# mLSTM attention feeding an FFN on one core: selection a slot earlier, exponents queued behind squares and x copies, state product and splits queued behind y

## The chip, the cores and the metric

The kernel runs on one core of a Trainium2 chip. The metric is device time of one execution in microseconds (us). The engines are named as in the profile: PE (TensorE, matmuls), PEld (its weight loads), DVE (VectorE), ACT (ScalarE), POOL (GpSimd) and SP (SyncE, whose queue issues the DMAs). A line such as L80 in a row of the profile is the line of a helper that issues the instruction, so the tiles' names tell the rows apart.

## The reference

Two steps follow each other. The first is a recurrent attention (mLSTM) over 4 batches, 8 heads, 768 positions and a head size of 40. For each position it does

```python
m_new = max(f + m, i)
C = exp(f + m - m_new) * C + exp(i - m_new) * outer(v, k)
n = exp(f + m - m_new) * n + exp(i - m_new) * k
y = sigmoid(o) * (C @ q) / max(abs(n . q), 1)
```

The second takes y, laid out as x with 3072 tokens of 320 columns, through `h = x @ w_in` (320 x 2048), a gate `g` that is h where h >= 1, 0 where h <= -1 and (h + 1)^2 / 4 between, and `g @ w_out` (2048 x 320).

## The kernel before

**Attention.** The positions are cut into 6 chunks of 128. A block n is one batch of one chunk, n = 4 * chunk + batch, so there are 24 blocks. Within a chunk the recurrence becomes matmuls: a decay matrix per head, made from sums of gates, is multiplied with the scores k.q, and the product with v; what came before the chunk enters through the state C. The work of a block is written as generators, which the program advances by a slot each:

- `prep(n)` (line 475): `select` sets the upper triangle of the block's tile Abc (128 x 8 heads x 128) to -30000 with an affine_select on POOL. `decay(n, hh)` (line 492) then takes the exponents of four heads, hh = 0 and 1, on ACT, eight instructions of 128x128 in all. `scale1` makes v1 on POOL, and the next block's v is loaded.
- `score(n)`: eight matmuls into two tiles psa, each multiplied into Abc by DVE; v2 on POOL.
- `main(n)` (line 569): PE multiplies the state with qn, DVE makes hv from it, then PE multiplies Abc with v1. For n >= 8, but not for the last batch of a chunk, both are first split into three bf16 parts by `parts3` (line 149): DVE writes what is left of v1 (v3) and of Abc (m3) after the first part, POOL what is left after the second, and PE does 96 small matmuls. DVE adds up into hv. Here `load_A(n + 3)` issues the load of a later block's Abc from a_d; the tiles Abc have three buffers. In the next slot DVE does z (two steps), its reciprocal, sz and y, and `carry_on` (line 544) makes the next state: PE multiplies v2 and k into psa, DVE masks the product into a tile C, POOL decays the old C, DVE adds the two. In a last slot PE transposes y, ACT casts it to xh, and DVE writes the rest to xl and to rows of xh.

**FFN.** The x of four blocks, one chunk, is X[j] with 512 tokens. An iteration x = 16 * j + fc takes one group of 128 of the 2048 columns. `mm1` does eight matmuls into psh (two buffers); ACT takes a Relu and a square into r; DVE makes r the gate, which frees psh. `parts` casts r to gh on ACT and writes the rest to gl on DVE. Two iterations later `mm2` does up to twelve matmuls from gh and gl into the four tiles pso. The iteration x = 16 * j can't begin before the last block of chunk j has been cast to xh; so x = 32 and x = 48 wait for the blocks 11 and 15. Its outputs are copied out by ACT and DVE.

**What sets the order.** The program calls the slots of the attention between the FFN's iterations: `plan` (line 643) puts prep, score and main of a block at slots that a list OFFS gives, 4 (LEAD) slots ahead of the score for prep and 3 (MLAG) behind it for main. A chunk's sigmoid of the output gate is called at its first main. Within this a scheduler sets each engine's queue. `behind(...)` (line 416) adds edges to it: an instruction issued under `behind("r", "act")` stands on its engine behind the last instruction that was marked so. The marks that exist before are ("r", "act"), the last square on ACT; ("r", "dve"), the last gate on DVE; ("x", "act"), the last cast to xh; ("x", "dve"), the last rest; and ("v", "pool"). An edge bears only on the order in a queue; each engine runs its own queue in order. The pool of tiles psa has two buffers, that of Abc three.

Of the kernel before, what the change touches and what calls it, by code (L numbers as in the profile page):

```python
# [13 lines left out]
ALU = mybir.AluOpType  # L14
# [3 lines left out]
B, H, S, D = 4, 8, 768, 40  # L18
D1 = D + 1
# [23 lines left out]
LEAD = 4  # L43
MLAG = 3
NA = 3
ST = 0


# [48 lines left out]
def mlstm_ffn_kernel(ctx, tc, qk, qn, vk, og, fi0, fi, w_in, w_out, cst, out):  # L97
    nc = Core(tc)
# [24 lines left out]
    bmask = cs_t.rearrange("p (g x) -> p g x", g=3)  # L123
# [25 lines left out]
    def parts3(x, name, eng):  # L149


        halves = lambda w: w.bitcast(BF16).rearrange("p h (t w) -> p h t w", w=2)
        hi = halves(x)[:, :, :, 1]
        rest = late.tile(list(x.shape), F32, name=name, bufs=1)
        eng[0].tensor_tensor(out=rest, in0=x, in1=hi, op=ALU.subtract)
        mid, lo = halves(rest)[:, :, :, 1], halves(rest)[:, :, :, 0]
        eng[1].tensor_tensor(out=lo, in0=rest, in1=mid, op=ALU.subtract)
        return hi, mid, lo
# [231 lines left out]
    mark = {}  # L390
# [25 lines left out]
    def behind(*names, only=True):  # L416
        es = ExitStack()
        for k in names:
            if only and k in mark:
                es.enter_context(tc.issue_after(mark[k].ins))  # L420
        return es
# [53 lines left out]
    def prep(n):  # L475

        c, b = divmod(n, B)
        t = T[n]
        select(n)
        for hh in range(2):  # L480
            decay(n, hh)
            yield
        scale1(n)
        load_v(n + 1)
        yield

    def select(n):
        A = T[n]["A"]
        nc.gpsimd.affine_select(out=A, in_=A, pattern=[[0, H], [1, L]], compare_op=ALU.is_ge,
                                fill=-30000.0, base=0, channel_multiplier=-1)  # L490

    def decay(n, hh):

        c, b = divmod(n, B)
        A = T[n]["A"]
        for h in range(4 * hh, 4 * hh + 4):
            bias = nA[:, c, b * H + h:b * H + h + 1]
            src = T[n]["Ap"][hh][:, (h - 4 * hh) * L:][:, :L] if c == 0 else A[:, h, :]
            nc.scalar.activation(A[:, h, :], src, AF.Exp, bias=bias)
# [44 lines left out]
    def carry_on(n, t):  # L544

        c, b = divmod(n, B)
        kp = psum_a()
        for gi, h0 in enumerate(GROUPS):
            nc.tensor.matmul(kp[0:120, gi * 3 * D1:(gi + 1) * 3 * D1], t["kn"][:, h0 * D:(h0 + 3) * D],
                             t["v2"][:, h0:h0 + 3, :], start=True, stop=True)  # L550
        Cn = st.tile([120, 3, 3 * D1], F32, name="C", bufs=5)
        nc.vector.tensor_tensor(out=Cn, in0=kp[0:120, :9 * D1].rearrange("p (g x) -> p g x", g=3),
                                in1=bmask, op=ALU.mult)
        if c > 0:
            C = state[b]
            nc.gpsimd.tensor_tensor(out=C, in0=C, in1=dec[:, :, b, c:c + 1].broadcast_to([120, 3, 3 * D1]),
                                    op=ALU.mult)
            nc.vector.tensor_tensor(out=Cn, in0=Cn, in1=C, op=ALU.add)
        state[b] = Cn
# [9 lines left out]
    def main(n):  # L569

        c, b = divmod(n, B)
        t = T.pop(n) if n >= B else T[n]
        g = gates_of(n)
        sg = sig[c][:, b, :]
        M = t["A"]
        if c > 0:
# [6 lines left out]
            hv = wk.tile([P, H, D1], F32, name="hv", bufs=2)  # L583
# [4 lines left out]
        if n < SPLIT_FROM or b == B - 1:  # L588
            for h in range(H):
                nc.tensor.matmul(up[:, h * D1:(h + 1) * D1], M[:, h, :], t["v1"][:, h, :], start=True, stop=True)  # L590
        else:
            prod = [(i, k) for i in range(3) for k in range(3 - i)]
            v = parts3(t["v1"], "v3", (nc.vector, nc.gpsimd))
            for h in range(H):
                if h % 8 == 0:
                    m = parts3(M[:, h:h + 8, :], "m3", (nc.vector, nc.gpsimd))
                for i, k in prod:
                    nc.tensor.matmul(up[:, h * D1:(h + 1) * D1], m[i][:, h % 8, :], v[k][:, h, :],
                                     start=((i, k) == (0, 0)), stop=((i, k) == (2, 0)))
# [3 lines left out]
        else:  # L603
            hv = uv
# [8 lines left out]
        sz = wk.tile([P, H, D], F32, name="sz", bufs=1)  # L613
        nc.vector.tensor_tensor(out=sz, in0=sg.rearrange("p (h d) -> p h d", d=D),
                                                     in1=z.unsqueeze(2).broadcast_to([P, H, D]), op=ALU.mult)
        y = wk.tile([P, DM], F32, name="y", bufs=2)
        nc.vector.tensor_tensor(out=y.rearrange("p (h d) -> p h d", d=D), in0=hv[:, :, 0:D], in1=sz, op=ALU.mult)
        if 0 < c < NC - 1:
            carry_on(n, t)
        yield  # L620
# [8 lines left out]
        j, r = divmod(n, NTC)  # L629
        if r == 0:  # L630
# [8 lines left out]
                                op=ALU.subtract)  # L639
# [4 lines left out]
    for n in range(NS):  # L644
        j, r = divmod(n, NTC)
        s0 = FRONT + OFFS[n - B] if j else 0
        if j:
            todo = ("prep", s0 - (LEAD if j > 1 else LEAD - 1), 3), ("score", s0, 2), ("main", s0 + MLAG, 3)
        else:
            todo = ("first", FRONT + ST + n, 2),  # L650
        for kind, i0, k in todo:
            for i in range(k):
                plan.setdefault(i0 + i, []).append((n, kind))
# [241 lines left out]
```

## Time and profile before

| | |
|---|---|
| time, median of three runs (lowest to highest) | 540.07 us (538.07 to 540.72) |
| the profiled execution's own time | 538.07 us |
| its span, from the first to the last instruction | 536.3 us |
| granted PE clock, mean | 0.958 of full speed |
| PE waits for psh, from DVE r | 12.2 us in 4 waits, longest 6.8 |
| PE waits for psa, from DVE y | 4.5 us in 2 waits, longest 2.3 |
| PE waits for psa, from DVE xh | 2.4 us in 2 waits, longest 1.9 |
| PE waits for psh, from ACT xh | 1.9 us in 2 waits, longest 0.9 |
| PE's share of the chain that ended last | 75% |

The rows that the prediction quotes are of three kinds. A row of a timeline reads: start in us, length in us, engine, line, operation, tile written <- tiles read, shapes, count, and in brackets the idle time of the engine just before it with what ended it. Instructions of one kind that follow each other share a row. A row of the table by stretches reads: the stretch, its length, the busy time (and number of instructions) of PE, PEld, DVE, ACT and POOL in it, then the granted clock of PE, the busy share of the DMA engines and GB/s. The page's first line gives busy time, its share of the span, and the number of instructions of each engine.

### The profile page before, as it was taken

Reading aid. Unit: us, or ns where it says so; the run is one execution under the profiler, and the core shown is the slowest. Engines: PE = TensorE matmul, PEld = TensorE weight load, DVE = VectorE, ACT = ScalarE, POOL = GpSimd, SP = SyncE. Lnnn points to the kernel's source line nnn. Section 1 sums busy time; section 2 is a strip of 40 time slices with the busy share of each in tenths; the row PEclk is TensorE's granted clock in tenths of the full one; section 3 lists DMA queues with packets and bytes.
Section 4 is the critical chain, followed back from the end, with each engine's and each line's share of the span. In section 5 each row is a group of like instructions: output and inputs, shape, how many; then the busy total and the mean of one; then the engine's idle time right before and its main releaser. Section 6 shows DMA issues by size and latency. Waiting matters only on the chain.

```text
span 536.3 us, 8899 instructions
## 1 busy us (share of the span) xinstructions
PE 501.1 (93%) x3396; PEld 427.1 (80%) x3399; DVE 359.7 (67%) x669; ACT 291.5 (54%) x576; POOL 138.8 (26%) x140
## 2 busy tenths in 40 slices
PE   8957999798997999969999979999999999999996
PEld 5735777676786889958888967988988889989986
DVE  5799997678675687748567558885566755544342
ACT  6544964555267464546636527663668444446553
POOL 3147423233352132223131232431231310000000
PEclk9987999899797999988999988999999999999999
DMA  8859454442441123233221233322243000010001
GB/s 245 264 188 303 129 172 146 149 153 91 142 134 19 41 63 103 79 88 93 51 87 56 80 113 120 74 90 77 68 149 135 19 1 2 0 38 13 1 1 50
DMA packets 29647, 51.30 MB, mean 96 GB/s; under 512 B 10124, under 2 KB 20004, under 8 KB 29604
## 3 DMA queue, kind: packets, MB, share of 16 engines
q1 hardware_dynamic: 29604, 50.72, 30.5%
q8 instruction: 27, 0.44, 0.4%
q14 instruction: 16, 0.13, 0.1%
HBM read 46.67 MB, written 4.04 MB: 95 GB/s over the span
## 4 chain that ended last, share of the span: by engine, by line
PE 75%; DVE 7%; ACT 7%; issue 3%; POOL 3%; DMA 3%; SPq 0%; ACTq 0%; POOLq 0%; DVEq 0%
PE psh L80 31%; PE pso L80 27%; PE psa L80 13%; ACT Abc L80 3%; POOL Abc L80 2%; PE psa L83 2%; DMA Abc<-a_d 2%; ACT r L80 1%; PE pso L83 1%; POOL v L80 1%; DVE r L80 1%; PE psh L83 1%; DVE win L80 1%; DVE ow L80 1%; DMA wraw<-in_w_out 1%
## 5 line engine op out<-in xcount | busy, mean ns | idle before, releaser
L80 ACT ACTIVATE r<-psh,half 128x512 f32<-128x512 f32 x96 | 65.2, 684 | 103.2 <-PE psh L80 102.9
L80 PE MATMUL psh<-xh,wh 128*128 128x512 f32 x288 | 107.4, 429 | 14.8 <-DVE r L80 12.2
L80 DVE SCALAR_TENSOR_TENSOR r<-psh,r 128x512 f32<-128x512 f32 x96 | 65.7, 686 | 80.6 <-ACT r L80 80.0
L80 PE MATMUL psh<-xh,wl 128*128 128x512 f32 x288 | 103.6, 414 | 0.0
L80 PE MATMUL pso<-ow,gh 128*128 128x320 f32 x320 | 99.4, 313 | 0.0
L80 PE MATMUL pso<-oh,gh 128*128 128x320 f32 x320 | 99.3, 313 | 0.0
L80 PE MATMUL pso<-oh,gl 128*128 128x320 f32 x320 | 93.3, 313 | 0.0
L80 DVE TENSOR_TENSOR gl<-r,gh 128x512 fp32r<-128x512 f32 x80 | 60.5, 758 | 32.4 <-ACT gh L80 31.9
L80 ACT CAST gh<-r 128x512 fp32r<-128x512 f32 x80 | 49.5, 618 | 48.9 <-DVE r L80 48.5
L80 PEld LDWEIGHTS psh<-xh,wh 128*128 128x128 f32 x288 | 53.1, 199 | 24.9 <-DVE r L80 13.9
L80 ACT ACTIVATE Abc<-Abc,nA 128x128 f32<-128x128 f32 x160 | 49.3, 390 | 37.3 <-POOL Abc L80 37.3
L80 PEld LDWEIGHTS psh<-xh,wl 128*128 128x128 f32 x288 | 56.7, 199 | 14.0 <-DVE m L83 0.4
L80 PEld LDWEIGHTS pso<-ow,gh 128*128 128x128 f32 x320 | 60.7, 190 | 3.4
L80 PEld LDWEIGHTS pso<-oh,gh 128*128 128x128 f32 x320 | 60.7, 190 | 3.3
L80 PE MATMUL psh<-xl,wh 128*128 128x512 f32 x192 | 62.7, 410 | 0.0
L80 ACT ACTIVATE r<-r 128x512 f32<-128x512 f32 x96 | 60.2, 631 | 2.4
L80 PEld LDWEIGHTS pso<-oh,gl 128*128 128x128 f32 x320 | 58.2, 188 | 0.8
L80 POOL TENSOR_TENSOR v<-vk,G 128x328 f32<-128x328 f32 x36 | 29.7, 829 | 67.2 <-issue 43.7
L80 PEld LDWEIGHTS psh<-xl,wh 128*128 128x128 f32 x192 | 37.6, 197 | 8.5
L80 POOL TENSOR_TENSOR C<-C,dec 120x369 f32<-120x369 f32 x16 | 13.7, 856 | 111.0 <-PE psa L80 111.0
L80 PE MATMUL pso<-ow,r 128*128 128x320 f32 x128 | 39.3, 452 | 0.0
L80 DVE TENSOR_TENSOR Abc<-psa,Abc 128x512 f32<-128x512 f32 x40 | 25.9, 680 | 17.8 <-PE psa L80 17.8
(187 smaller groups left out, 728.2 us busy)
## 6 DMA issues: line engine op xcount, KB each, us to landing
Abc<-a_d SPq DMA_DIRECT2D x20, 512.0 KB
raw<-in_qk SPq DMA_DIRECT2D x48, 160.0 KB
vk<-in_vk SPq DMA_DIRECT2D x20, 324.0 KB
wraw<-in_w_in SPq DMA_DIRECT2D x8, 768.0 KB
wraw<-in_w_out SPq DMA_DIRECT2D x8, 640.0 KB
sig<-in_og SPq DMA_DIRECT2D x6, 640.0 KB
out<-r SPq DMA_DIRECT2D x24, 160.0 KB
qn<-in_qn SPq DMA_DIRECT2D x20, 180.0 KB
```

The source lines that it names most:

```text
L80: r = getattr(self.engine, name)(*args, **kwargs)
L83: r = getattr(self.engine, name)(*args, **kwargs)
```

## The change

Blocks 4 to 7 (JOINED) keep their selection and exponents in one slot. For all other blocks `prep` starts a slot earlier and does only the selection in its first slot, so that the exponents keep their slots. The exponents are issued behind the last square and the last cast to xh on ACT. The masked state product and the splits v3 and m3 are issued behind the last y on DVE.

```diff
--- before.py
+++ after.py
@@ -43,6 +43,8 @@
 LEAD = 4
 MLAG = 3
 NA = 3
+
+JOINED = (4, 5, 6, 7)
 ST = 0
 
 
@@ -477,8 +479,11 @@
         c, b = divmod(n, B)
         t = T[n]
         select(n)
+        if n not in JOINED:
+            yield
         for hh in range(2):
-            decay(n, hh)
+            with behind(("r", "act"), ("x", "act")):
+                decay(n, hh)
             yield
         scale1(n)
         load_v(n + 1)
@@ -549,8 +554,9 @@
             nc.tensor.matmul(kp[0:120, gi * 3 * D1:(gi + 1) * 3 * D1], t["kn"][:, h0 * D:(h0 + 3) * D],
                              t["v2"][:, h0:h0 + 3, :], start=True, stop=True)
         Cn = st.tile([120, 3, 3 * D1], F32, name="C", bufs=5)
-        nc.vector.tensor_tensor(out=Cn, in0=kp[0:120, :9 * D1].rearrange("p (g x) -> p g x", g=3),
-                                in1=bmask, op=ALU.mult)
+        with behind("y"):
+            nc.vector.tensor_tensor(out=Cn, in0=kp[0:120, :9 * D1].rearrange("p (g x) -> p g x", g=3),
+                                    in1=bmask, op=ALU.mult)
         if c > 0:
             C = state[b]
             nc.gpsimd.tensor_tensor(out=C, in0=C, in1=dec[:, :, b, c:c + 1].broadcast_to([120, 3, 3 * D1]),
@@ -590,10 +596,12 @@
                 nc.tensor.matmul(up[:, h * D1:(h + 1) * D1], M[:, h, :], t["v1"][:, h, :], start=True, stop=True)
         else:
             prod = [(i, k) for i in range(3) for k in range(3 - i)]
-            v = parts3(t["v1"], "v3", (nc.vector, nc.gpsimd))
+            with behind("y"):
+                v = parts3(t["v1"], "v3", (nc.vector, nc.gpsimd))
             for h in range(H):
                 if h % 8 == 0:
-                    m = parts3(M[:, h:h + 8, :], "m3", (nc.vector, nc.gpsimd))
+                    with behind("y"):
+                        m = parts3(M[:, h:h + 8, :], "m3", (nc.vector, nc.gpsimd))
                 for i, k in prod:
                     nc.tensor.matmul(up[:, h * D1:(h + 1) * D1], m[i][:, h % 8, :], v[k][:, h, :],
                                      start=((i, k) == (0, 0)), stop=((i, k) == (2, 0)))
@@ -614,7 +622,7 @@
         nc.vector.tensor_tensor(out=sz, in0=sg.rearrange("p (h d) -> p h d", d=D),
                                                      in1=z.unsqueeze(2).broadcast_to([P, H, D]), op=ALU.mult)
         y = wk.tile([P, DM], F32, name="y", bufs=2)
-        nc.vector.tensor_tensor(out=y.rearrange("p (h d) -> p h d", d=D), in0=hv[:, :, 0:D], in1=sz, op=ALU.mult)
+        mark["y"] = nc.vector.tensor_tensor(out=y.rearrange("p (h d) -> p h d", d=D), in0=hv[:, :, 0:D], in1=sz, op=ALU.mult)
         if 0 < c < NC - 1:
             carry_on(n, t)
         yield
@@ -645,7 +653,8 @@
         j, r = divmod(n, NTC)
         s0 = FRONT + OFFS[n - B] if j else 0
         if j:
-            todo = ("prep", s0 - (LEAD if j > 1 else LEAD - 1), 3), ("score", s0, 2), ("main", s0 + MLAG, 3)
+            lead = (LEAD if j > 1 else LEAD - 1) + (n not in JOINED)
+            todo = ("prep", s0 - lead, 3 + (n not in JOINED)), ("score", s0, 2), ("main", s0 + MLAG, 3)
         else:
             todo = ("first", FRONT + ST + n, 2),
         for kind, i0, k in todo:
```

What this does to the queues is shown at three places. In the rows a number behind a name tells the tiles of one name apart; the numbers of later tiles differ by up to three between the two kernels.

The first is ACT around x = 32, before. Abc_2130 is block 14, xh_1615 the x of chunk 2 (its fourth cast is block 11's), r_2365 belongs to x = 32, sig_2132 is chunk 3's output gate, and x8 counts instructions of one kind in a row:

```order
L80 ACTIVATE ex_2162<-ah_2160 32x128
L80 ACTIVATE Abc_2130<-Abc_2130,nA_122 128x128 x8
L80 CAST xh_1615<-psa_2231 128x3x128
L80 ACTIVATE r_2365<-psh_2356,half_118 128x512
L80 ACTIVATE r_2403<-psh_2394,half_118 128x512
L80 COPY r_2498<-pso_1379 128x320
L80 ACTIVATE r_2365<-r_2365 128x512
L80 ACTIVATE r_2403<-r_2403 128x512
L80 ACT_TABLE_LOAD
L80 ACTIVATE sig_2132<-sig_2132 128x1280
L80 CAST gh_2375<-r_2365 128x512
```

and after:

```order
L82 CAST xh_1615<-psa_2231 128x3x128
L82 ACTIVATE Abc_1989<-Abc_1989,nA_122 128x128 x8
L82 ACTIVATE r_2365<-psh_2356,half_118 128x512
L82 ACTIVATE r_2406<-psh_2397,half_118 128x512
L82 COPY r_2498<-pso_1379 128x320
L82 ACTIVATE r_2365<-r_2365 128x512
L82 ACTIVATE r_2406<-r_2406 128x512
L82 ACT_TABLE_LOAD
L82 ACTIVATE sig_2132<-sig_2132 128x1280
L82 ACT_TABLE_LOAD
L82 ACTIVATE Abc_2130<-Abc_2130,nA_122 128x128 x4
L82 CAST gh_2378<-r_2365 128x512
```

The cast of block 11's x no longer stands behind eight exponents. Abc_1989 (block 13) now stands behind it, and half of block 14's exponents behind the sigmoid, with a table load between, ahead of the cast gh_2378.

The second is DVE ahead of x = 32, before. C_2190 is the state after block 11, v3 belongs to block 12, and hv, z, sz and y to block 11:

```order
L80 SCALAR_TENSOR_TENSOR ah_2160<-rst_128,fi_t_2157 32x128
L80 TENSOR_TENSOR gl_2334<-r_2321,gh_2332 128x512
L80 TENSOR_TENSOR hv_2118<-psa_2120,hv_2118 128x328
L80 TENSOR_TENSOR C_2190<-psa_2186,cs_99 120x369
L80 TENSOR_TENSOR v3_2414<-v1_2194 128x328
L80 SCALAR_TENSOR_TENSOR z_2178<-hv_2118,G_121 128x8
L80 TENSOR_TENSOR C_2190<-C_2190,C_1297 120x369
L80 TENSOR_TENSOR z_2178<-z_2178,hv_2118 128x8
L80 RECIPROCAL z_2178<-z_2178 128x8
L80 TENSOR_TENSOR sz_2182<-sig_1241,z_2178 128x320
L80 TENSOR_TENSOR y_2184<-hv_2118,sz_2182 128x320
L80 TENSOR_TENSOR xl_1616<-psa_2231,xh_1615 128x2x128
```

and after:

```order
L82 TENSOR_TENSOR hv_2118<-psa_2120,hv_2118 128x328
L82 SCALAR_TENSOR_TENSOR ah_2160<-rst_128,fi_t_2157 32x128
L82 TENSOR_TENSOR gl_2334<-r_2321,gh_2332 128x512
L82 SCALAR_TENSOR_TENSOR z_2178<-hv_2118,G_121 128x8
L82 TENSOR_TENSOR z_2178<-z_2178,hv_2118 128x8
L82 RECIPROCAL z_2178<-z_2178 128x8
L82 TENSOR_TENSOR sz_2182<-sig_1241,z_2178 128x320
L82 TENSOR_TENSOR y_2184<-hv_2118,sz_2182 128x320
L82 TENSOR_TENSOR C_2190<-psa_2186,cs_99 120x369
L82 TENSOR_TENSOR v3_2417<-v1_2194 128x328
L82 TENSOR_TENSOR C_2190<-C_2190,C_1297 120x369
L82 TENSOR_TENSOR xl_1616<-psa_2231,xh_1615 128x2x128
```

hv moves ahead of a scan (ah) and of gl_2334; the mask of C, v3 and the addition of C move from ahead of z, sz and y to behind y.

The third is ACT at the start of attention chunk 2, before. sig_1241 is its output gate, Abc_1239 block 10, Abc_1494 block 11, and gh_1407 the first cast behind the sigmoid:

```order
L80 ACT_TABLE_LOAD
L80 ACTIVATE sig_1241<-sig_1241 128x1280
L80 CAST oh_133<-ow_611 128x640
L80 CAST gh_1407<-r_1397 128x512
L80 COPY r_1521<-pso_533 128x320
L80 CAST gh_1504<-r_1428 128x512
L80 ACTIVATE ex_1269<-ah_1267 32x128
L80 ACT_TABLE_LOAD
L80 ACTIVATE Abc_1494<-Abc_1494,nA_122 128x128 x3
L80 ACTIVATE r_1539<-psh_1530,half_118 128x512
L80 ACTIVATE Abc_1494<-Abc_1494,nA_122 128x128 x5
L80 ACTIVATE r_1539<-r_1539 128x512
```

and after:

```order
L82 ACTIVATE sig_1241<-sig_1241 128x1280
L82 ACT_TABLE_LOAD
L82 ACTIVATE Abc_1239<-Abc_1239,nA_122 128x128 x4
L82 CAST oh_133<-ow_611 128x640
L82 CAST gh_1410<-r_1397 128x512
L82 COPY r_1521<-pso_533 128x320
L82 CAST gh_1504<-r_1431 128x512
L82 ACTIVATE ex_1269<-ah_1267 32x128
L82 ACTIVATE r_1539<-psh_1530,half_118 128x512
L82 ACTIVATE r_1604<-psh_1595,half_118 128x512
L82 ACTIVATE r_1539<-r_1539 128x512
L82 ACTIVATE Abc_1239<-Abc_1239,nA_122 128x128 x4
```

A table load and four exponents of block 10 stand directly behind the sigmoid, ahead of the casts of oh and of gh. The exponents of block 11 are gone from between this chunk's Relu and square of r_1539, and the other four of block 10 stand in their place, behind that square.

Elsewhere: the eight exponents of block 9 move from ahead of a Relu (r_1363) to behind two later casts of xh. At the start of chunk 4 four exponents stand ahead of the second square and four behind sigmoid and table load; at that of chunk 5 eight. At the start of x = 48 the same holds for C, v3 and y of block 15 as for block 11. On DVE at the start of chunk 2, y, v3, m3 and C stand ahead of the gate of r_1539, where C and y stood behind it. On POOL the selection passes the low part of v3. On SP some loads swap places.

## The prediction, made before the run

> **What bounds the kernel now.** The page's busy times come first. They name the bound:
>
> ```profile
> PE 501.1 (93%) x3396; PEld 427.1 (80%) x3399; DVE 359.7 (67%) x669; ACT 291.5 (54%) x576; POOL 138.8 (26%) x140
> ```
>
> Of a span of 536.3 us TensorE is busy for 501.1, so it stands idle for 35.2, and no change of order can give more than this and whatever busy time runs at a low clock. The second view is the table by stretches, which shows the granted clock (the last figure but two) beside PE's busy time:
>
> ```profile
> 133.20:140.00 6.80, 6.80 (x23) 5.37 (x23) 5.96 (x12) 0.08 (x1) 3.62 (x4) 0.50 0.46 149
> 164.00:170.80 6.80, 5.99 (x18) 5.19 (x19) 5.96 (x13) 4.44 (x9) 0.20 (x1) 0.50 0.04 8
> 228.80:232.20 3.40, 1.33 (x7) 0.96 (x8) 1.36 (x3) 2.81 (x9) 0.11 (x1) 1.00 0.50 137
> 232.20:235.60 3.40, 3.40 (x10) 2.63 (x9) 0.30 (x2) 0.00 (x0) 0.00 (x0) 0.50 0.15 56
> 239.10:242.50 3.40, 2.22 (x15) 1.61 (x14) 3.40 (x4) 3.37 (x6) 3.16 (x2) 1.00 0.72 227
> 242.50:245.90 3.40, 3.40 (x10) 2.57 (x9) 2.61 (x8) 2.40 (x5) 1.05 (x2) 0.50 0.16 52
> 317.60:321.00 3.40, 3.30 (x8) 2.62 (x9) 0.72 (x2) 0.05 (x1) 0.00 (x0) 0.50 0.33 123
> 327.80:331.20 3.40, 3.40 (x18) 2.92 (x16) 3.36 (x9) 3.37 (x6) 0.15 (x1) 0.50 0.28 88
> 340.00:410.00 70.00, 70.00 (x553) 62.10 (x552) 47.76 (x89) 41.45 (x84) 18.90 (x20) 1.00 0.29 96
> ```
>
> From 340 to 410 us PE is busy all the time at clock 1.00, so nothing can be won there. Before that there are stretches of 3.4 us, or two of them, at clock 0.50. Those whose forerunner is shown follow a stretch in which PE stood idle for over a microsecond: 2.07 of 3.40 us before 232.20, 1.18 before 242.50. A stretch at half clock does half its work, so it costs 1.7 us, and a double one 3.4. An idle gap is thus paid twice where it is long enough.
>
> A page of the Trainium skill, "TensorE: Matmul & The Clock Gate", section "HAM oscillation — how this bites in real kernels", gives the rule that PE should have no idle gaps over about 3.4 us. By it most of these stretches would have no cause; the trace does not agree, since 1.18 us of idle time in a stretch of 3.4 was followed by the half clock, and I go by the trace.
>
> The third view is PE's timeline around two starts of a chunk of tokens, x = 32 and x = 48, where new x must be ready before the FFN can go on:
>
> ```profile
> 227.44 0.31 PE L80 MATMUL pso<-oh,gl 128*128 128x320 f32 x1
> 229.92 0.52 PE L80 MATMUL psa<-ident,y 128*128 128x128 f32 x3 [2.17 <-DVE y L80]
> 231.80 0.88 PE L80 MATMUL psh<-xh,wh 128*128 128x512 f32 x2 [0.94 <-ACT xh L80]
> 315.83 0.52 PE L80 MATMUL psa<-ident,y 128*128 128x128 f32 x3 [2.31 <-DVE y L80]
> 317.70 1.22 PE L80 MATMUL psh<-xh,wh 128*128 128x512 f32 x2 [0.94 <-ACT xh L80]
> ```
>
> At both PE waits twice: for y (2.17 and 2.31 us), then for the cast of x to xh (0.94 each). Between the waits lie only the transposes and two score matmuls.
>
> **The change, part by part.** No instruction's kind or size changes, and the ACT_TABLE_LOADs of the order stay 12. All that moves is queue order.
>
> *y ahead of the state product and the splits, at x = 32.* DVE's and ACT's rows there:
>
> ```profile
> 223.66 0.41 DVE L80 TENSOR_TENSOR_SCAN ah<-rst,fi_t 32x128 f32<-32x128 f32 x1
> 224.12 1.03 DVE L80 TENSOR_TENSOR gl<-r,gh 128x512 fp32r<-128x512 f32 x1
> 225.08 0.48 DVE L80 TENSOR_TENSOR hv<-psa,hv 128x328 f32<-128x328 f32 x1
> 225.49 0.53 DVE L80 TENSOR_TENSOR C<-psa,cs 120x369 f32<-120x369 f32 x1
> 225.93 0.48 DVE L80 TENSOR_TENSOR v<-v 128x328 f32<-128x328 f32 x1
> 226.42 0.53 DVE L80 TENSOR_TENSOR C<-C 120x369 f32<-120x369 f32 x1
> 229.28 0.49 DVE L80 TENSOR_TENSOR y<-hv,sz 128x320 f32<-128x320 f32 x1
> 228.94 2.45 ACT L80 ACTIVATE Abc<-Abc,nA 128x128 f32<-128x128 f32 x8 [4.52 <-POOL Abc L80]
> 231.29 0.45 ACT L80 CAST xh<-psa 128x384 fp32r<-128x384 f32 x1
> ```
>
> Neighbours overlap by some 0.08 (v3 starts 0.44 after C, which is 0.53 long), so C mult, v3 and C add take 0.53 + 0.48 + 0.53 less 0.24: 1.30. The changed order also puts hv ahead of the scan and of gl, 223.66 to 225.08: 1.42. Together y ends 2.72 earlier, at 229.77 − 2.7 = 227.1. PE is done with its own work at 227.75, so the wait of 2.17 goes. Then comes the cast. Before, it starts as the eight exponents release ACT (228.94 + 2.45 = 231.39), although the transposes were over at 230.44. In the changed order these exponents (block 14) stand a chunk start later, and the ones that stand here (block 13) come behind the cast. So the cast follows the transposes at once and lies beside the two score matmuls. Transposes and score matmuls took PE from 229.92 to 231.80 − 0.94 = 230.86, that is 0.94; 227.75 + 0.94 is 228.7 for the first psh, against 231.80: −3.1. The idle time left in that stretch is under 0.3, below the 1.18 that was followed by half clock, so the stretch at 232.20 should run at full clock: −1.7. What is late next is the C product, behind y: it starts at about 227.1 in place of 225.49 and holds a psa buffer 1.6 longer; the score matmuls want that buffer at 228.2, when it is free by half a microsecond, so I count nothing; if that cover is gone it costs at most those 1.6.
>
> *The same at x = 48.* 317.70 becomes 314.55 by the same steps (2.31 + 0.94, less 0.1 of remaining wait): −3.15, and the stretch at 317.60: −1.7.
>
> *Block 9's exponents.* At 129 us they hold ACT before Relu and the xh cast:
>
> ```profile
> 126.52 2.44 ACT L80 ACTIVATE Abc<-Abc,nA 128x128 f32<-128x128 f32 x8 [1.53 <-POOL Abc L80]
> 130.72 0.47 ACT L80 CAST xh<-psa 128x384 fp32r<-128x384 f32 x1
> 129.15 0.49 PE L80 MATMUL psa<-ident,y 128*128 128x128 f32 x3
> 132.20 2.02 PE L80 MATMUL psa<-v,Abc 128*128 128x41 f32 x13 [1.93 <-DVE xh L80]
> ```
>
> Afterwards they stand behind this xh cast and the next. The Relu, square and cast between them then move up by up to 2.44, but the xh cast can't start before the transposes end at 129.64, so it gains 130.72 − 129.67 = 1.05 of the 1.93. An idle rest of 0.88 is less than the 1.18 seen, yet the half clock of 133.20 to 140.00 is open, so its 3.4 goes into the range and not into the sum: −1.05.
>
> *Exponents behind squares, at the three starts of attention chunks 2, 3 and 4.* Here the new order speaks against the change. ACT at the start of chunk 2, and what PE takes from it:
>
> ```profile
> 152.15 1.28 ACT L80 ACT_TABLE_LOAD   x1
> 153.44 1.28 ACT L80 ACTIVATE sig<-sig 128x1280 f32<-128x1280 f32 x1
> 155.24 0.62 ACT L80 CAST gh<-r 128x512 fp32r<-128x512 f32 x1
> 157.19 0.31 PE L80 MATMUL pso<-oh,gh 128*128 128x320 f32 x1
> 164.81 1.22 PE L80 MATMUL psh<-xh,wh 128*128 128x512 f32 x2 [3.30 <-DVE r L80]
> ```
>
> Behind the sigmoid now stand a table load and four exponents, ahead of the cast of gh. A load is 1.28 by its row, four exponents half of 2.44 to 2.45, so 1.25: gh is ready 2.5 later, at 158.4, where PE wants it at 157.2. A new wait of 1.2 is born. But the eight exponents of block 11 no longer stand ahead of the square of the next r. A copy, a gh, an ex, two Relus and the square follow at some 0.5 each (gh is 0.62 long), so ACT has that square by about 161.4. DVE, whose last gl waits for the second gh, reaches y at about 161.0 and has y, v3, m3 and C ahead of r: by the rows above 0.49, 0.48 and 0.53, and some 1.4 for m3, which has three times v3's columns; 161.0 + 2.8 + 0.6 for r is 164.4 where PE could go on at 164.81. The two waits together are 0.4 shorter: −0.4 net, and between −3.3, if DVE's order is kinder, and +1.2, if only the new wait is left over. The half clock from 164.00 stays.
>
> The Trainium skill's page "ScalarE: Activation LUTs", section "What ACT_TABLE_LOAD costs", puts a switch at about 2.66 us, 1.28 for the load and 1.38 for draining. By it three loads moved ahead of casts would cost up to 4.1 us more, and the sum below would be some 4 us smaller. The trace does not show that drain: sig starts 1.29 after the load, and I keep 1.28.
>
> The starts of chunks 3 and 4 look alike, with the casts and the matmuls that wait for them here:
>
> ```profile
> 243.31 0.60 ACT L80 CAST gh<-r 128x512 fp32r<-128x512 f32 x1
> 246.56 0.31 PE L80 MATMUL pso<-oh,gh 128*128 128x320 f32 x1
> 326.91 0.72 PE L80 MATMUL psh<-xh,wh 128*128 128x512 f32 x2 [1.26 <-DVE r L80]
> 329.14 0.60 ACT L80 CAST gh<-r 128x512 fp32r<-128x512 f32 x1
> 331.17 0.41 PE L80 MATMUL pso<-oh,gh 128*128 128x320 f32 x1
> ```
>
> Chunk 3: 243.91 + 2.5 is 246.4, at PE's 246.56. The first matmul is met, the next casts are as late and not all are: between 0 and 2.5, I take 1.0. Chunk 4: four more exponents stand ahead of the second square and the sigmoid, so gh ends at 329.74 + 3.8 = 333.5, where PE wants it at 331.17 and, with 0.7 of a longer wait at 326.91 behind m3, at 331.9. The two make 2.3; a score or state product in PE's queue fills some, so I take 1.9, between 0.7 and 2.5. The half clocks at 242.50 and 327.80 stay. At chunk 5 and at the FFN's later starts the same casts stand behind the same load and up to eight exponents (1.28 + 2.45 = 3.7), but they lie past 340 us, where PE never waits by the row above: between 0 and 3.7, I take 0, nearest to that row.
>
> *Selection a slot earlier.* It starts when its load has landed, not when it is issued:
>
> ```profile
> 151.64 0.33 SPq L80 DMA_DIRECT2D Abc<-a_d  x1
> 155.73 4.72 POOL L80 TENSOR_SCALAR_AFFINE_SELECT Abc<-Abc 128x1024 f32<-128x1024 f32 x1 [3.17 <-DMA Abc<-a_d]
> ```
>
> By itself it is worth nothing; in POOL's order it only passes the low part of v3. That part then ends later by a select, up to 4.7 us; the split products that read it stand later in PE's queue: nothing, at most the 1.0 that I already count at chunk 3.
>
> *Before 125 us* exponents move behind squares and Relus in the same way as for block 9, some with gain and some with loss: I count nothing, ±1.05 by block 9's term.
>
> **Sum.** −3.1 − 1.7 − 3.15 − 1.7 − 1.05 − 0.4 + 1.0 + 1.9 = −8.2. The profiled execution took 538.07 (1.77 around its span), so 529.9. It was the fastest of three; their median stands 2.0 above. For the changed kernel I add half of that: 531.0.
>
> **The rivals.**
>
> *More stretches at full clock.* If the shorter gap at 132.20 no longer brings the half clock (3.4), and one stretch each at 242.50 and 327.80 goes too (1.7 each), 531 becomes 524. For it: half clock follows idle time, and the idle time falls. Against it: two of the three get new waits.
>
> *The casts become the wait, and it ends slower.* ACT runs its queue in order, so load and exponents stand ahead of the cast of gh at a chunk's start. If five starts pay the full 2.5 (12.5), and the first three one more stretch at half clock (5.1), that is +17.6 against gains of −3.1 − 1.7 − 3.15 − 1.7 − 1.05 = −10.7, so +6.9 on 539.1 (the profiled time and the 1.0): 546. With three of the five (7.5) it is +1.9: 541. It decides where PE reaches the first pso matmul less than 2.5 us after the old end of gh. For it: 157.19 and 331.17 do. Against it: 246.56 just not, and past 340 us there is no wait to show that PE is close behind its casts.
>
> *The change does not do what it says.* The select is bound to the landing of its load, and y stays late since DVE waits for main's products (hv needs PE), so only half of the two waits at x = 32 and 48 goes (−3.2) and the clock stays low there; block 9's exponents gain nothing either: −3.2 − 0.4 + 2.9 = −0.7, about 538.4. For it: hv started at 225.08 right behind gl, so the row does not show when its input was ready.
>
> **Chances.** Half a per cent, 2.7 us, is about what can be told from no change. The forecast has 0.56, more full clock 0.12, casts late 0.15, little done 0.17. The first two are faster, so 0.68; the fourth is the same, 0.17; the third slower, 0.15. The forecast's own range is 526 to 536. To hold 8 in 10 the range goes from 523, just past the fast rival, to 540, past the fourth; the slow one stays out.
>
> **What would show it.** Right: at x = 32 and 48 PE's waits for y and xh under 0.3 us and those two stretches at clock 1.00; DVE's y ahead of C; the xh cast directly behind the transposes. Right on the costs: new waits of PE for gh at three starts, 1 to 2 us each. Wrong: waits for gh of 2.5 or more with a half clock behind them, or PE waiting at x = 32 and 48 for something else.

## The result, and the profile after

The changed kernel takes 523.70 us (median of four runs), the kernel before 539.07 on the same chip: a ratio of 0.9707, 95% interval 0.9653 to 0.976. One of the four runs, at 533.02 us, was slow; it counts in the median but not in the ratio. The profiled execution took 522.81 us; its span is 521.0 against 536.3. The page's first line answers to the one shown of before:

```profile
PE 493.2 (95%) x3396; PEld 419.9 (81%) x3399; DVE 355.5 (68%) x669; ACT 291.5 (56%) x576; POOL 144.3 (28%) x140
```

PE's idle time falls from 35.2 to 27.8 us, and its busy time by 7.9 although it does the same work. The second is work that now runs at a higher clock. PE's timeline of the changed kernel, at the places where the prediction showed its waits (columns as before):

```profile
132.39 1.95 PE L82 MATMUL psa<-v,Abc 128*128 128x41 f32 x16 [0.79 <-DVE xh L82]
157.49 0.41 PE L82 MATMUL pso<-oh,gh 128*128 128x320 f32 x1 [0.51 <-ACT gh L82]
162.62 0.73 PE L82 MATMUL psh<-xh,wh 128*128 128x512 f32 x2 [1.04 <-DVE r L82]
222.71 0.49 PE L82 MATMUL psa<-ident,y 128*128 128x128 f32 x3
223.77 0.74 PE L82 MATMUL psh<-xh,wh 128*128 128x512 f32 x2 [0.15 <-ACT xh L82]
303.00 0.49 PE L82 MATMUL psa<-ident,y 128*128 128x128 f32 x3
304.06 0.73 PE L82 MATMUL psh<-xh,wh 128*128 128x512 f32 x2 [0.15 <-ACT xh L82]
311.78 0.73 PE L82 MATMUL psh<-xh,wh 128*128 128x512 f32 x2 [1.26 <-DVE r L82]
318.41 0.41 PE L82 MATMUL pso<-oh,gh 128*128 128x320 f32 x1 [0.59 <-ACT gh L82]
```

At x = 32 and 48 the wait for y is gone and 0.15 us is left of the wait for xh. The new waits at these places are the two for gh, 0.51 and 0.59. The table by stretches shows the granted clock (last figure but two) where it was 0.50 before, some with the stretch ahead of them:

```profile
132.16:135.57 3.41, 3.07 (x24) 2.79 (x24) 3.32 (x7) 0.01 (x1) 1.42 (x3) 1.00 0.27 65
135.57:138.98 3.41, 3.03 (x6) 2.05 (x7) 3.27 (x9) 0.00 (x0) 1.37 (x2) 0.50 0.84 249
159.46:162.88 3.42, 2.38 (x17) 2.14 (x16) 3.42 (x7) 3.42 (x9) 3.42 (x3) 1.00 0.28 93
162.88:169.70 6.82, 6.82 (x37) 5.77 (x37) 6.71 (x12) 3.87 (x10) 2.04 (x2) 1.00 0.06 6
224.32:227.73 3.41, 3.41 (x25) 2.66 (x23) 0.38 (x2) 1.74 (x6) 0.34 (x1) 1.00 0.12 42
231.14:234.56 3.42, 3.20 (x13) 2.21 (x14) 3.42 (x6) 3.39 (x4) 2.02 (x3) 1.00 0.42 143
306.24:309.65 3.41, 3.41 (x27) 2.41 (x27) 1.62 (x4) 0.88 (x3) 0.00 (x0) 1.00 0.10 12
309.65:313.06 3.41, 2.15 (x21) 1.75 (x20) 3.22 (x5) 3.39 (x9) 1.90 (x1) 1.00 0.69 234
313.06:316.48 3.42, 3.42 (x62) 3.09 (x61) 3.16 (x8) 3.40 (x3) 1.40 (x2) 1.00 0.36 109
```

One stretch of 3.4 us at half clock is left past 130 us, where before there were eight (two double ones and four single).

Where the time came from is read from the start of the first psh matmul of an iteration x in the two traces:

| x | before | after | difference | gained since the row above | forecast for it |
|---|---|---|---|---|---|
| 0 | 31.31 | 33.60 | +2.29 | +2.29 | - |
| 14 | 121.04 | 122.36 | +1.32 | -0.97 | 0 ± 1.05 |
| 18 | 153.36 | 152.36 | -1.00 | -2.32 | -1.05 |
| 25 | 190.62 | 185.63 | -4.99 | -3.99 | -0.4 |
| 31 | 218.06 | 213.10 | -4.96 | +0.03 | 0 |
| 32 | 231.80 | 223.77 | -8.03 | -3.07 | -3.1 |
| 46 | 298.99 | 288.77 | -10.22 | -2.19 | -1.7 + 1.0 |
| 58 | 367.22 | 351.75 | -15.47 | -5.25 | -3.15 - 1.7 + 1.9 |
| 94 | 520.73 | 505.73 | -15.00 | +0.47 | 0 |

The late start of x = 0 is not of the change's making: in the run without the early selection below, whose queues are the same, x = 0 started at 31.19.

On DVE ahead of x = 32, y now ends at 221.87, a microsecond before PE's last pso matmul ends (222.87), and C, v3 and the C add follow it (some rows are left out):

```profile
218.83 0.48 DVE L82 TENSOR_TENSOR hv<-psa,hv 128x328 f32<-128x328 f32 x1
219.64 0.65 DVE L82 TENSOR_TENSOR gl<-r,gh 128x512 fp32r<-128x512 f32 x1
220.41 0.17 DVE L82 TENSOR_TENSOR z<-z,hv 128x8 f32<-128x8 f32 x1
220.85 0.49 DVE L82 TENSOR_TENSOR sz<-sig,z 128x320 f32<-128x320 f32 x1
221.38 0.49 DVE L82 TENSOR_TENSOR y<-hv,sz 128x320 f32<-128x320 f32 x1
221.78 0.54 DVE L82 TENSOR_TENSOR C<-psa,cs 120x369 f32<-120x369 f32 x1
222.64 1.43 DVE L82 TENSOR_TENSOR C<-C 120x369 f32<-120x369 f32 x1
```

On ACT the cast of x starts 0.04 us after the transposes end at 223.20, and the exponents come behind it (the view shown ends after five of the eight):

```profile
223.24 0.48 ACT L82 CAST xh<-psa 128x384 fp32r<-128x384 f32 x1 [3.19 <-PE psa L82]
223.61 1.57 ACT L82 ACTIVATE Abc<-Abc,nA 128x128 f32<-128x128 f32 x5
```

### The profile page after: what moved, and what is told of

The parts are those of the page before. It is cut to its first block, busy times and chain, and to the rows that moved or that the text cites. A ratio compares the mean times of both kernels' runs of the same rounds, so it can differ in the third digit from the quotient of the medians.

```text
span 521.0 us, 8909 instructions
## 1 busy us (share of the span) xinstructions
PE 493.2 (95%) x3396; PEld 419.9 (81%) x3399; DVE 355.5 (68%) x669; ACT 291.5 (56%) x576; POOL 144.3 (28%) x140
## 5 line engine op out<-in xcount | busy, mean ns | idle before, releaser
L82 PE MATMUL psh<-xh,wh 128*128 128x512 f32 x288 | 104.5, 419 | 10.1 <-DVE r L82 9.0
L82 PE MATMUL psh<-xh,wl 128*128 128x512 f32 x288 | 100.1, 401 | 0.0
L82 DVE TENSOR_TENSOR gl<-r,gh 128x512 fp32r<-128x512 f32 x80 | 62.3, 779 | 34.1 <-ACT gh L82 33.6
L82 PEld LDWEIGHTS psh<-xh,wh 128*128 128x128 f32 x288 | 51.2, 193 | 20.0 <-DVE r L82 10.9
L82 PEld LDWEIGHTS psh<-xh,wl 128*128 128x128 f32 x288 | 55.0, 192 | 13.3 <-DVE m L85 0.4
L82 PE MATMUL psh<-xl,wh 128*128 128x512 f32 x192 | 61.2, 400 | 0.0
L82 POOL TENSOR_TENSOR v<-vk,G 128x328 f32<-128x328 f32 x36 | 32.0, 894 | 60.1 <-issue 33.6
L82 POOL TENSOR_SCALAR_AFFINE_SELECT Abc<-Abc 128x1024 f32<-128x1024 f32 x20 | 26.7, 1339 | 44.9 <-DMA Abc<-a_d 29.2
```

The costliest lines, as they stand in the source:

```text
L82: r = getattr(self.engine, name)(*args, **kwargs)
```

## The experiments

The theory at the start was that of the prediction: two queues have to be free at x = 32 and 48, DVE's for y and ACT's for the cast of x, and the half clock follows PE's idle time. The first three kernels take the change apart, the fourth tests the clock.

**y alone.** Against the changed kernel:

```diff
-JOINED = (4, 5, 6, 7)
+JOINED = tuple(range(4, 24))
...
-            with behind(("r", "act"), ("x", "act")):
-                decay(n, hh)
+            decay(n, hh)
```

> The kernel before with only the state product and the splits queued behind y. Theory (queues): y alone does not pay, since ACT still holds the cast of x. At x = 48 the cast is free of exponents in this order and y is early, so PE's first psh there comes some 3 us earlier and the stretch at half clock behind it goes: -4.9. At x = 32 this order puts eight exponents, which wait for a selection, ahead of the cast gh that PE needs first: +2.5 or more. Sum -2.5 to +1 us. Rival (y is what pays, at both places alike): -9 to -10 us, PE without a wait over 0.3 us at both.

Measured: 526.17 us, ratio 0.98 to before, interval 0.9757 to 0.9843. That is the rival's size, -10 us, not the theory's, though PE's waits of over 0.3 us are not gone. PE's waits at the two places:

```profile
225.24 0.42 PE L82 MATMUL pso<-oh,gh 128*128 128x320 f32 x1 [1.27 <-ACT gh L82]
306.70 0.52 PE L82 MATMUL psa<-ident,y 128*128 128x128 f32 x3 [0.79 <-DVE y L82]
307.79 0.73 PE L82 MATMUL psh<-xh,wh 128*128 128x512 f32 x2 [0.15 <-ACT xh L82]
```

At x = 32 PE waits 1.27 us for gh (the exponents stand ahead of it, as expected) but not for y or xh; at x = 48 0.79 for y and 0.15 for xh. The exponents at x = 32 were over in time, because the selection came earlier than I had reckoned: it started at 220.85 here, and the first psh matmul of x = 32 at 226.53. So the theory fell in this form; what brought the selection forward is read below, behind the run with the selection first.

**Exponents alone.** The other way round: JOINED as above and the three `with behind("y")` taken out.

> The kernel before with only the exponents queued behind squares and casts of x. Theory (queues): the start of chunk 2 gains as in the changed kernel, about 4 us, block 9 some 1 to 3; at x = 32 and 48 the cast of x follows the transposes but y is late, so only 0.9 each is won and the half clock stays: -6 to -8 us in all against before. Rival (the exponents' order is the whole gain): -14 to -16 us, and no PE wait over 0.3 us at x = 32 and 48.

Measured: 534.33 us, ratio 0.9969, interval 0.9937 to 1.0001: not told from no change. PE's timeline shows why:

```profile
223.62 0.52 PE L82 MATMUL psa<-ident,y 128*128 128x128 f32 x3 [1.64 <-DVE y L82]
306.09 0.52 PE L82 MATMUL psa<-ident,y 128*128 128x128 f32 x3 [1.27 <-DVE y L82]
397.93 0.74 PE L82 MATMUL psh<-xh,wh 128*128 128x512 f32 x2 [1.55 <-DVE r L82]
471.94 1.01 PE L82 MATMUL psh<-xh,wh 128*128 128x512 f32 x2 [2.46 <-DVE r L82]
```

Up to x = 58 this kernel's trace is 12.3 us ahead of before, more than expected. Then it gives 8.5 back, of which the two new waits for r (x = 66 and 82) are 4.0 and the stretch at half clock behind the second of them 1.7; the rest was not traced. At the end it is 3.8 ahead. Past 340 us, where I had said that nothing can be won, it can be lost.

**No early selection.** JOINED as above and nothing else, so that no block's selection gets a slot of its own. All five queues are row for row those of the changed kernel.

> The changed kernel without the selection a slot earlier (every block joined). Its queues are row for row those of the changed kernel on all five engines. Theory (queues): the same time as the changed kernel, 522 to 525 us. Rival (the earlier slot itself is worth something): 527 us or more.

Measured: 524.31 us, ratio 0.9757, interval 0.9678 to 0.9836; its profiled span is 521.0, that of the changed kernel. The interval by itself would just allow the rival's 527; with the same rows in all queues there is nothing left that could make it. A third of the change in its code does nothing: the scheduler puts the selections where it put them without it.

**Filling the waits.** The kernel before with matmuls that nobody reads:

```diff
+        if n in (11, 15):
+            if True:
+                for _ in range(8):
+                    nc.tensor.matmul(xp, wh[:, 0, :P], wh[:, 0, :512], start=True, stop=True)
         for k in range(2):
             nc.tensor.transpose(xp[:, k * P:(k + 1) * P], y[:, k * P:(k + 1) * P], ident)
-        nc.tensor.transpose(xp[:, 2 * P:3 * P], y[:, DM - P:], ident)
+        mark["tr"] = nc.tensor.transpose(xp[:, 2 * P:3 * P], y[:, DM - P:], ident)
...
+        if fc == 0 and j in (2, 3):
+            with behind("tr"):
+                for _ in range(5):
+                    nc.tensor.matmul(hp, wh[:, 0, :P], wh[:, 0, :512], start=True, stop=True)
```

> The kernel before with 13 extra matmuls of 128x512 on PE at each of x = 32 and 48, 8 in the wait for y and 5 in the wait for the cast of x; they compute nothing that is used. Theory (clock): the waits stay as long, but PE is busy in them, so the stretches behind them run at clock 1.00: -1.7 us each, -3.4 us in all. Rival (the low clock has another cause, or the extra matmuls cost as much as they save): 0 or slower, granted clock 0.50 still there behind x = 32 and 48.

Measured: 536.01 us, ratio 0.9979, interval 0.994 to 1.0018. As a time that is the rival. But the table by stretches shows clock 1.00 behind both places, and after the later waits for m3 and r as well, while the untouched place at 163 us keeps its half clock:

```profile
162.89:169.72 6.83, 5.86 (x17) 5.04 (x18) 5.93 (x13) 4.60 (x9) 0.38 (x2) 0.50 0.03 8
230.00:233.40 3.40, 3.40 (x15) 2.36 (x13) 0.72 (x2) 0.42 (x2) 0.00 (x0) 1.00 0.47 158
233.40:240.00 6.60, 5.42 (x39) 4.40 (x39) 5.55 (x8) 4.66 (x7) 3.33 (x2) 1.00 0.41 130
240.00:247.00 7.00, 6.88 (x76) 5.98 (x76) 4.63 (x11) 6.01 (x11) 2.14 (x2) 1.00 0.15 52
316.40:319.80 3.40, 3.19 (x16) 2.40 (x17) 0.72 (x2) 0.16 (x1) 0.00 (x0) 1.00 0.38 140
319.80:333.00 13.20, 10.83 (x115) 9.09 (x114) 11.60 (x20) 10.14 (x17) 3.81 (x3) 1.00 0.35 106
```

Against before this trace gains 3.0 us from x = 31 to 36 and 1.6 from x = 48 to 51 with the waits as long as ever. It gives 2.9 back from x = 37 to 40, where the extra rows moved others in the queues and PE waits for r:

```profile
259.33 0.73 PE L80 MATMUL psh<-xh,wh 128*128 128x512 f32 x2 [2.67 <-DVE r L80]
```

So where the waits were filled the half clock is gone. The 4.6 us gained are those of four stretches, and only two of them lie behind a filled wait; the two behind the waits for m3 and r went without being filled, so what filling alone is worth isn't shown by this trace. The kernel's time as a whole shows no gain. All traces taken together, at the end of this document, bear out that long idle time brings the half clock.

The next two part what is behind y. The new theory (theory 2) was that the splits held the selection: on POOL the selection of a later block stood behind the low part of v3, which waits for v3 on DVE.

**Splits alone.** The kernel of y alone, with the state product back in its old place.

> The kernel before with only the splits v3 and m3 queued behind y; the state product is left where it was. In this order the selection stands ahead of the low part of v3 on POOL, as in the run with y alone. Theory 2 (the selection was held by v3 on POOL, and through it the exponents and the cast of x): nearly all of what y alone brought, 8 to 11 us faster than before. Rival (y itself is ready sooner, by C as much as by v3): 3 to 6 us faster.

Measured: 526.43 us, ratio 0.9812, interval 0.9764 to 0.9861: the whole gain of y alone. C still stands ahead of y here, and at x = 32 y is in time all the same; PE waits there only for gh, 1.29 us. At x = 48 it still waits 0.99 for y.

**State product alone.** The kernel of y alone, with v3 and m3 back.

> The kernel before with only the masked state product queued behind y; v3 and m3 are left where they were, and on POOL the selection still stands behind the low part of v3. Theory 2 (the selection held by v3): at x = 32 the exponents still stand ahead of the cast of x, so 0 to 2 us faster than before, PE's two waits there still 2 us or more together and the half clock behind them. Rival (y ready sooner is what pays): 4 to 6 us faster.

Measured: 539.77 us, ratio 1.0046, interval 1.0006 to 1.0085: slower, if anything, where 0 to 2 us faster was expected. Up to x = 58 its trace is 2.2 us ahead of before; it loses that later, in part to a new wait of 2.21 us for y at 407.11 with 6.8 us at half clock behind it. PE's, ACT's, SP's and POOL's rows at x = 32:

```profile
226.64 0.52 PE L82 MATMUL psa<-ident,y 128*128 128x128 f32 x3 [0.17 <-DVE y L82]
230.34 1.22 PE L82 MATMUL psh<-xh,wh 128*128 128x512 f32 x2 [2.76 <-ACT xh L82]
```

```profile
227.48 2.44 ACT L82 ACTIVATE Abc<-Abc,nA 128x128 f32<-128x128 f32 x8 [4.55 <-POOL Abc L82]
229.83 0.45 ACT L82 CAST xh<-psa 128x384 fp32r<-128x384 f32 x1
```

```profile
222.29 0.34 SPq L82 DMA_DIRECT2D Abc<-a_d  x1
224.89 0.74 POOL L82 TENSOR_TENSOR v<-v 128x328 bf16<-128x328 f32 x1 [0.52 <-DVE z L82]
226.08 1.37 POOL L82 TENSOR_SCALAR_AFFINE_SELECT Abc<-Abc 128x1024 f32<-128x1024 f32 x1 [0.45 <-DMA Abc<-a_d]
```

Here is the case that I had expected of y alone: the wait for y is down from 2.17 to 0.17, and the wait for xh grows from 0.94 to 2.76, since the cast still stands behind exponents that wait for their selection. Both queues do have to be free, and without the exponents' edge it is the splits, not C, whose place frees the second. But POOL's rows speak against theory 2: the low part of v3 is done at 225.63, and the selection still waits 0.45 us, for the load of its tile.

**Selection first.** To see whether the place of the splits on DVE matters, the kernel before with the selection of blocks from 10 on called ahead of v3 of the block two before, where that is split, and no more in `prep`; nothing stands behind y:

```diff
+            if n + 2 >= 10 and n + 2 < NS and (n + 2) % 4 != 1:
+                select(n + 2)
             v = parts3(t["v1"], "v3", (nc.vector, nc.gpsimd))
...
-        eng[1].tensor_tensor(out=lo, in0=rest, in1=mid, op=ALU.subtract)
+        with behind("sel" if name == "v3" else "none"):
+            eng[1].tensor_tensor(out=lo, in0=rest, in1=mid, op=ALU.subtract)
```

> The kernel before with nothing behind y and no exponents moved by hand; only the selection of the block two ahead is called ahead of v3, and v3's low part stands behind it on POOL. C and v3 stay ahead of y on DVE. In this order PE's products of block 11 also stand some 12 rows earlier. Theory 3 (what counts is that the last block's products, and with them the selection and the exponents, come earlier, not C's and v3's place on DVE): 5 to 9 us faster than before, the two waits at x = 32 under 1.5 us together. Rival (it is the splits' place behind y on DVE): 0 to 2 us faster.

Measured: 529.76 us, ratio 0.9858, interval 0.98 to 0.9916: -7.6 us by the ratio, within the range of theory 3. The two waits at x = 32 are 1.04 for y and 0.53 for xh, 1.57 together and so just over what was expected. In its order, as in those of the splits and of y alone, PE's products of block 11 stand earlier, so that the load of block 14's tile goes out earlier too; the selection ran at 221.10 and the exponents at 222.90, ahead of the cast at 225.25.

What held the selection at x = 32 can be read from the traces of these runs. The load of block 14's tile overwrites the tile that block 11's products read:

| run | block 11's products on PE stand | they end | load goes out | low part of v3 ends | selection starts | after the load's issue |
|---|---|---|---|---|---|---|
| before | behind the psh matmuls of x = 31 and 12 pso matmuls | 223.55 | 223.58 | 227.55 | 227.81 | 4.23 |
| exponents alone | the same | 217.71 | 217.77 | 221.84 | 221.98 | 4.21 |
| state product alone | the same | 222.26 | 222.29 | 225.63 | 226.08 | 3.79 |
| changed | 6 rows earlier | 217.72 | 217.79 | behind the selection | 222.22 | 4.43 |
| selection first | 12 rows earlier | 217.21 | 217.25 | behind the selection | 221.10 | 3.85 |
| y alone | ahead of the psh matmuls of x = 31 | 216.95 | 216.98 | behind the selection | 220.85 | 3.87 |
| splits alone | the same | 215.10 | 215.14 | behind the selection | 219.09 | 3.95 |

The load always goes out within 0.07 us of the end of those products, and the selection starts 3.8 to 4.4 us after that, whether the low part of v3 stands ahead of it or behind. So POOL's order was worth a few tenths of a microsecond at most here, and theory 2 has the wrong holder, although its forecast for splits alone came true. What moved the selection, the exponents and the cast is that in the orders with the splits behind y the scheduler also puts block 11's products earlier on PE. Why it does so was not looked into.

At the start of chunk 2 the splits bear on a selection in another way. In the kernel before, the selection took 4.72 us beside DVE's work, and the exponents that stand ahead of a square waited 2.16 us for it; with the state product alone it is 4.62 and 2.16. With splits alone, where the split m3 no longer runs beside it, the selection takes 3.18, the exponents wait 0.61, and PE's wait for r falls from 3.30 to 1.42. In the changed kernel these exponents no longer stand there.

**gh ahead of the exponents.** The prediction's cost was the cast of gh behind table load and exponents. An edge takes it away from the changed kernel:

```diff
-        nc.scalar.copy(gh, r)
+        mark["gh"] = nc.scalar.copy(gh, r)
...
-            with behind(("r", "act"), ("x", "act")):
+            with behind(("r", "act"), ("x", "act"), "gh"):
                 decay(n, hh)
```

> The changed kernel with one more edge: the exponents also stand behind the last cast gh on ACT, so that at the chunks' starts gh comes ahead of the table load and the four exponents. Theory (queues): PE's waits for gh of 0.51 us at 157 and 0.59 us at 318 go, 0.5 to 1.3 us faster than the changed kernel, 522 to 524 us. Rival (the exponents, one cast later, are late for the scores or for the next square): no faster, and new PE waits for Abc or r of a microsecond or more.

Measured: 519.76 us, ratio 0.969, interval 0.9637 to 0.9743. The time is below what was expected, on another chip; by the ratios (0.969 against 0.9707) it is 0.9 us faster than the changed kernel. To set it beside the changed kernel on one chip both ran again, with a third that also puts the state product back:

> The changed kernel once more, beside the next two on one chip: 522 to 526 us, 0.97 to 0.976 of before.

Measured: 521.64 us, ratio 0.972, interval 0.9655 to 0.9785: the ratio as expected, the time just under.

> The changed kernel with gh ahead of the exponents once more, beside the changed kernel on one chip: 1 to 5 us faster than it, no PE wait for gh at 150 to 160 or 310 to 320 us.

Measured: 519.75 us, ratio 0.9673, interval 0.962 to 0.9727. ACT takes gh first now, and PE's waits for gh are gone from its timeline. The wait for r at x = 25 grows from 1.04 to 1.40. ACT's rows:

```profile
149.67 1.28 ACT L82 ACTIVATE sig<-sig 128x1280 f32<-128x1280 f32 x1
150.85 0.71 ACT L82 CAST oh<-ow 128x640 fp32r<-128x640 f32 x1
151.46 0.62 ACT L82 CAST gh<-r 128x512 fp32r<-128x512 f32 x1
152.10 1.28 ACT L82 ACT_TABLE_LOAD   x1
```

> The changed kernel with gh ahead of the exponents, and the state product back in its old place (only the splits stand behind y). The state product alone behind y made the kernel before 0.5% slower. Theory (queues: C behind y is a cost that the rest hides): 0 to 2 us faster than gh first alone. Rival (C behind y is needed for y to be in time at x = 32): 1 to 3 us slower than gh first alone, PE waiting for y there.

Measured: 519.98 us, ratio 0.9678, interval 0.9623 to 0.9732: the same as gh first alone. PE does wait for y at x = 32 here, 0.84 us, as the rival said, but the time doesn't show it. With the exponents and the splits in their new places C's place makes no difference to the time that was seen, for or against. The two kernels with gh first had the lowest medians of all, 1.9 and 1.7 us under the changed kernel on the same chip, but the intervals overlap. In the traces the kernel with gh first alone draws ahead of the changed kernel's second profile from x = 50 to 58 (by 1.6 us), where that profile has a stretch at half clock (309.60) and PE waits for gh in neither; so the edge is not shown to be the cause.

## Why the prediction was right and wrong

The direction was right, and the time, 523.70, lies at the low end of the range. The case that came true is not the forecast (531) but the rival with more stretches at full clock, which stood at 524 and was given 0.12. That its sum came out is in part luck: of its three places, the stretches at 242.50 and 327.80 went, the double one at 133.20 went by half, and the double one at 164.00, which it left standing, went whole. The table above says where:

- *y and the cast at x = 32 and 48.* Right in size: -3.07 against -3.1 at x = 32, and the two waits at x = 48 fell from 3.25 to 0.15, as forecast. Both stretches behind them ran at full clock, as forecast. For the cast the working was right too: it follows the transposes, and the exponents come behind it. For y the size was right by luck. Against the end of PE's last pso matmul y ended 3.0 us earlier (2.02 behind it before, 1.00 ahead of it now); the forecast had 2.72, from 1.30 for C, v3 and the C add, and 1.42 for hv passing the scan ah and gl. The 1.42 is a mistake: in the changed order ah and gl still stand ahead of z, sz and y, and hv's input had been ready since 223.55, so hv's place can't bring y forward.
- *The lengths of gl, z and sz were taken as fixed.* This made up for the mistake. DVE's rows before, and POOL's beside the second:

```profile
226.87 0.70 DVE L80 TENSOR_TENSOR z<-z,hv 128x8 f32<-128x8 f32 x1
227.84 1.41 DVE L80 TENSOR_TENSOR sz<-sig,z 128x320 f32<-128x320 f32 x1
```

```profile
227.81 1.09 POOL L80 TENSOR_SCALAR_AFFINE_SELECT Abc<-Abc 128x1024 f32<-128x1024 f32 x1 [0.27 <-DMA vk<-in_vk]
```

  In the changed kernel no selection runs beside sz, and it takes 0.49; z takes 0.17, and gl 0.65 where it took 1.03. Before, POOL worked beside z (the low part of v3, 226.50 to 227.55) and beside gl (v, 223.78 to 225.75) too. The C add, which took 0.53, now lies beside the selection (from 222.22) and takes 1.43. The Trainium skill's page "SBUF — State Buffer", section "SBUF: two separate sides", has DVE and POOL share a pair of ports that one instruction holds whole; these rows agree. Together that is 1.8 us of y's earlier end that I did not count: 1.3 from the order and 1.8 from these rows make the 3.1 us by which the way from the copy of carry on DVE (223.55 before, 218.76 now) to y's end is shorter.
- *Block 9's exponents.* Right: the wait fell from 1.93 to 0.79, by 1.14 against 1.05. Of the double stretch behind it one half went, which I had left to the range.
- *"The half clock from 164.00 stays."* This step failed, and is the largest miss: -3.99 from x = 18 to 25, where I had -0.4. The two waits sum to 0.51 + 1.04 = 1.55 against 3.30; I had 2.9. For gh I had 1.2: it came when forecast, at 157.43 in a trace that is 1.0 ahead, but PE now does the state product (0.80 us from 156.19) before it asks for gh. For r I had 1.7: DVE came to y at 159.50, half a microsecond sooner than forecast, and m3 took 1.21 and not 1.4. The two waits lie in different stretches of 3.41 us, and neither was followed by half clock. With y alone, splits alone and exponents alone the iterations from 18 or 19 to 25 or 26 gain about as much, 4.2 to 4.6 us, and in each of them the wait for r there is under 1.5 us; with C alone it is 3.29, and they gain 1.2.
- *"The half clocks at 242.50 and 327.80 stay."* This failed too in the profiled run. In the changed kernel's second profile the one at x = 50 was there, so it hangs on little.
- *The casts of gh.* The mechanism was right and the sizes too large: 0.51 at chunk 2 (1.2 forecast), 0.17 for gl and none for gh at chunk 3 (1.0), 0.59 at chunk 4 (1.9, with 0.7 of it for r, which waited 1.26 as before). With gh first these waits go.
- *"Selection a slot earlier: by itself nothing."* Right: the queues are the same without it. Its passing the low part of v3 on POOL is worth little too, as I had it ("nothing, at most 1.0"): at x = 32 the selection starts 3.8 to 4.4 us after its load goes out in either order. What the prediction did not see is that the splits' place also moves block 11's products on PE, and the load with them. By time the splits' place alone brought 10 of the 13 to 16 us; by the traces at x = 58 the exponents' place alone had brought 12.3 as well, of which it kept 3.8.
- *Past 340 us: nothing.* Right for this kernel (+0.47). The runs with the exponents alone and with the state product alone show that it need not be.

## What to carry to other kernels

Where an order edge moves one instruction, compare the queues of all engines and not only the one that it names: here an edge for two splits on DVE came with earlier products on PE, and with these an earlier load, selection, exponents and cast. Before naming what holds an instruction, look at what it waits for last: the selection stood behind a split on POOL, but it waited for its load. Take the parts of such a change one at a time, since a part can be worth nothing in the queues (the earlier selection) or nothing by itself (the state product). When adding up what an instruction's new place saves, count what still stands ahead of it. A wait of PE pays twice when it goes and takes a stretch at half clock with it, so the clock of each stretch belongs in the sum as a case of its own and not as a constant.

## What the runs showed of the hardware

Idle time alone does not tell when the granted clock drops. In the changed kernel's profile PE stood idle for 1.26 of 3.41 us at 309.65 and ran at 1.00 afterwards; in the second profile of the same kernel 1.25 idle at the same place was followed by 0.50:

```profile
306.18:309.60 3.42, 2.17 (x21) 1.56 (x20) 3.23 (x5) 3.34 (x9) 1.31 (x1) 1.00 0.59 199
309.60:313.01 3.41, 3.41 (x12) 2.73 (x10) 3.38 (x8) 3.38 (x4) 0.59 (x1) 0.50 0.31 112
```

And the stretch at 132.16 above, idle for only 0.34 but mostly taken up by matmuls of 41 columns, was followed by 0.50. How much PE streams in a stretch, and not only whether it is busy, may be what counts; no run here was made to settle it.

Over the thirteen traces, from 95 us on and counted in the stretches of 3.41 us between which the clock changes, long idle time did tell: all 16 stretches at full clock with 1.87 us or more of it were followed by half clock. Of 53 with 1.0 to 1.8 us, 17 were.

POOL's and DVE's instructions stretch beside each other. A selection of 128x1024 took 1.09 us in the kernel before at 227.81, where DVE's sz, which started 0.03 later, took the longer time, and 4.72 at 155.73, where DVE worked without a pause.
